# Attention with beacon keys and a quick-GELU MLP: order of the first loads, engine of the first masks, share of the copies

## The chip, the core and the metric

The kernel runs on one core of a Trainium2 chip. The core has a matmul engine (TensorE, PE in the profile), a vector engine (VectorE, DVE), a scalar engine for exp, GELU and copies (ScalarE, ACT), a general engine (GpSimd, POOL) and a queue engine that only issues transfers (SyncE, SP). Each runs its own list of instructions in order and waits for the others by semaphores. DMA transfers can be issued by SyncE, ScalarE and GpSimd; those of GpSimd may change the type on the way, from float32 in memory to float16 on the chip.

The metric is the time of one execution in microseconds. Before the change it is 367.99 us, the median of 5 runs (367.88 to 368.15).

## The reference

Eight batches, eight heads, 576 tokens of 64 features. Each head attends to 16 beacon keys, which every token sees, and causally to its own 576 keys. The result, all heads of a token side by side, goes through a two-layer MLP with x times sigmoid(1.702 x) between.

```python
B, H, S, Nb, D = (8, 8, 576, 16, 64)
k_all = concatenate([beacon_k, k], axis=2)
v_all = concatenate([beacon_v, v], axis=2)
scores = matmul(q, k_all.T) / sqrt(D)
scores = where(causal, -1e9, scores)        # beacon columns are never masked
a = exp(scores - scores.max(-1))
a /= a.sum(-1) + 1e-09
x = matmul(a, v_all)                        # to [B * S, H * D] = [4608, 512]
h = x @ w_in                                # 512 -> 2048
out = (h * sigmoid(1.702 * h)) @ w_out      # 2048 -> 512
```

## The kernel before, in words

**Pairs.** The unit of attention is a pair of heads: four pairs in each of eight batches, steps i = 0 to 31. For one pair, `qk_chunk` (L322) computes transposed scores (keys on partitions, queries along the row) in four chunks `CH` (L288), two heads each. `exp_chunk` (L340) turns a chunk into float16 weights E with ScalarE, and `mask_chunk` (L351) sets the weights above the diagonal to zero: one instruction for each of five diagonal blocks of a pair, on VectorE (a minimum with the tile `keep`) or on GpSimd (`affine_select`). Then TensorE multiplies E with V. A constant part of the V tile, set by `ones` (L100), makes row sums in the same way.

**Two ways to the normalized result.** The first four pairs (`NBOTH`) use `av_both` (L421), and VectorE reads the sums and products straight from PSUM (`z_turn_both`, `z_recip`, `z_back`, `norm_both`). Later pairs use `av_half` (L389); a copy `av_out` (L456) on VectorE or ScalarE takes the products out of PSUM, and VectorE does the rest (`z_turn`, `z_recip`, `z_back`, `norm`). The result is the MLP's input `xT`.

**q and k.** They are needed with features on partitions. For batches 0 and 1 they are loaded by `load_qk6` (L143), transposed by TensorE (`tr_pe`, L185) and copied out of PSUM (`tr_pe_out`, L196). In batch 0, heads 0 and 1 are an exception: `load_f32` (L151) loads them as float32 on the queues of SyncE (k) and ScalarE (q), and `cast_f32` (L162) makes float16 of them. Batches 2 to 7 are loaded by `load_qk` (L112), turned in 32 by 32 blocks on VectorE (`tr_squares`), put in order by VectorE or GpSimd (`tr_order`), written to memory and read back by SyncE (`tr_write`, `tr_place`).

**Beacons.** `load_bk6` (L170) and `cast_bk6` (L178) bring the beacon keys of batches 0 and 1; `load_bk` (L123, eight small transfers on SyncE) and `cast_bk` (L135) those of batches 2 to 7, at the kernel's start.

**MLP.** The 4608 tokens are nine groups of 512. `mlp1` (L511, matmuls at L516) makes 16 blocks of the hidden layer, each followed by a GELU on ScalarE; `mlp2` (matmuls at L538) makes four blocks of output, copied out by `mlp2_out` (L551 on VectorE, L549 on ScalarE) and stored by SyncE. Group g starts after the scores of pair `ends[g]` - 1, so the first group follows pair 4.

**What sets the order.** Every piece of work is a `Work` (L561) with the engines that may run it, a duration, a key (its due time in steps), the works it needs, and works that must start before it (`after`). `Buf` and `rings` (L573, L578) stand for the buffers in turn. `issue` (L964) is a planner that runs while the program is built: it takes again and again the work that could start first by its own clock, by key among equals, and for a work with several engines the one that would finish first, with a penalty `BIAS` (L765, L995) in microseconds: VectorE's is 0.5 up to its clock 45, ScalarE's 0.7 after. The order in which the works are taken is the program's order on each engine's list. So a changed duration or penalty can move any work. `first_loads` (L620) holds batches 0 and 1; the V loads are at L738, w_in and w_out at L744 and L745. Throw-away matmuls (`warm`, L1041) fill gaps of TensorE up to the planner's clock 60.

```python
c = (t, 0 if w.mode == mode == 1 else 1, w.key)
...
eng = min(w.opts, key=lambda e: max(t, free[e]) + w.opts[e] + BIAS[t > 45].get(e, 0))
```

Of the kernel before, what the change touches and what calls it, by code (L numbers as in the profile page):

```python
# [9 lines left out]
F16 = mybir.dt.float16  # L10
# [6 lines left out]
def kernel(  # L17
# [75 lines left out]

    w1t = cst.tile([P, NKP, DFF], F16, tag="w1", name="w1")
# [48 lines left out]
    def load_qk6(b, h0, h1, w):  # L143
        if b not in nat6:
            nat6[b] = gp.tile([TP, 2, H, TR * D], F16, tag="g", name="g")
        nc.gpsimd.dma_start(  # L146
            out=nat6[b][:, w, h0:h1, :],
            in_=(q, k)[w][b, h0:h1].rearrange("h (p t) d -> p h (t d)", t=TR),
        )

    def load_f32(w, eng):  # L151

        s = op_.tile([P, 2, S], F32, tag="O", name="O")
        stg[w] = s
        dict(SP=nc.sync, ACT=nc.scalar)[eng].dma_start(
            out=s.rearrange("p x s -> p (x s)")[0:TP, 0 : 2 * TR * D].rearrange(
                "p (h c) -> p h c", h=2
            ),
            in_=(q, k)[w][0, 0:2].rearrange("h (p t) d -> p h (t d)", t=TR),
        )  # L160

    def cast_f32(w, eng):  # L162
        if 0 not in nat6:
            nat6[0] = gp.tile([TP, 2, H, TR * D], F16, tag="g", name="g")
        copy[eng](
            out=nat6[0][:, w, 0:2, :].rearrange("p h c -> p (h c)"),
            in_=stg[w].rearrange("p x s -> p (x s)")[0:TP, 0 : 2 * TR * D],
        )
# [152 lines left out]

    def qk_chunk(i, ci):  # L322
        b, p = divmod(i, NPAIR)
        qT, kT = qTs[b % 2], kTs[b % 2]
        sc = pss.tile([P, 2, 512], F32, tag="s", name="s")
        scs[(i, ci)] = sc
        o = 0
        for (j, a, e) in CH[ci]:
            for x in range(2):
                r = 64 * x  # L330
                nc.tensor.matmul(  # L331
                    sc[:, x, o : o + e - a],
                    kT[r : r + 64, p, j * P : (j + 1) * P],
                    qT[r : r + 64, p, a:e],
                    start=True,
                    stop=True,
                )
            o += e - a
# [244 lines left out]
    SPL, CAP = 2.0, 2.0  # L583
    NBOTH = 4
# [9 lines left out]
    bkB = None  # L594
    pk = {}
    trp = {}
    mkeep = Work("POOL", 0.3, -4.95, make_keep)
    midn = Work("POOL", 0.6, -5.95, lambda: make_identity(nc, ident))

    bk6, stw, cst0 = {}, {}, {}  # L600
    stb = {w: Buf("O") for w in (1, 0, "bk")}
    stw[1] = Work("SP", 0.6, -9, lambda: load_f32(1, "SP"), alloc=stb[1], dma=0.7)
    stw[0] = Work("ACT", 0.6, -9, lambda: load_f32(0, "ACT"), alloc=stb[0], dma=0.7, after=[stw[1]])
    for b in range(NB2):
        ob = Buf("osb")
        x = Work("SP", 0.6, -8 + b, lambda b=b: load_bk6(b), alloc=ob, dma=0.1, after=[stw[1]])
        bk6[b] = Work(
            dict(ACT=0.6, DVE=0.6) if b else dict(ACT=0.6), 0, (-8, 1.5)[b],
            lambda eng, b=b: cast_bk6(b, eng), [x],
        )  # L610
        use(ob, bk6[b])
    g0 = Buf("g")
    for w in (1, 0):
        cst0[w] = Work(
            {("DVE", "ACT")[w]: 0.85}, 0, -8.5 - 0.1 * w, lambda eng, w=w: cast_f32(w, eng),
            [stw[w]],
        )
        use(stb[w], cst0[w])

    def first_loads(b):  # L620
        k0 = 4 * b
        kl = (-6, -4.4)[b]
        gb6 = g0 if b == 0 else Buf("g")
        lds = {(0, 1): cst0[1], (0, 0): cst0[0]} if b == 0 else {}
        got = []
        for (h0, h1) in ((2, 4), (4, H)) if b == 0 else ((0, 4), (4, H)):
            for w in (1, 0):
                x = Work(
                    "POOL", 0.7, kl + 0.1 * h0 + 0.02 * (1 - w) + (h0 == 4),
# [6 lines left out]
        if b == 0:  # L636
            for x in cst0.values():
                x.after.append(got[0])
# [31 lines left out]
        if b == 0:  # L670
            bk6[1].after.append(pk[(0, 0, 1)])

    for b in range(B):
# [5 lines left out]
        for g in range(2) if b >= NB2 else ():  # L679
            for w in (1, 0):  # L680
# [17 lines left out]
                for e in range(2):  # L698
                    cp.append(Work(
                        dict(DVE=0.8, POOL=1.3), 0, k0,  # L700
# [5 lines left out]
                if w == 1:  # L706
                    if bkB is None:
                        ld4 = [
                            Work(
                                "SP", 1.2, -6 + x, lambda x=x: load_bk(x),  # L710
                                alloc=stb["bk"] if x == 0 else None, dma=0.2,
# [3 lines left out]
                        for x, y in zip(ld4, ld4[1:]):  # L715
                            y.after.append(x)
                        bkB = [Work(dict(ACT=0.85, DVE=0.85, POOL=0.9), 0, 3, cast_bk, ld4)]
                        use(stb["bk"], *bkB)
# [46 lines left out]
    BIAS = dict(DVE=0.5), dict(ACT=0.7)  # L765
    avs = []
    evs = {}
    for i in range(NSTEP):
# [5 lines left out]
        for c in range(len(CH)):  # L774
            s_ = Buf("s")
            qk_ = Work(
                "PE", CHW[c] / 2400 + 0.05, i + (0, 0.01, 0.4, 0.41)[c],
                lambda i=i, c=c: qk_chunk(i, c),
                [pk[(b, p, 0)], pk[(b, p, 1)], pk[b]] if b < NB2
# [17 lines left out]
            mk = Work(  # L797
                dict(DVE=0.46 * nm, POOL=0.41 * nm), 0, i + 0.3,
                lambda eng, i=i, c=c: mask_chunk(i, c, eng), [ex, mkeep],
            )  # L800
            use(Eb, mk)
# [6 lines left out]
        if i < NBOTH:  # L808
            for z in (1, 0):
                for half in range(2):  # L810
# [4 lines left out]
                        "PE", sum(hi - lo for (j, lo, hi, col) in mm) / 2400 + 0.15,  # L815
                        i + 1.05 + 0.2 * (1 - z) + 0.1 * half,
                        lambda i=i, half=half, z=z: av_both(i, half, z),
                        [r for j in js for r in ready[j]] + vb_, alloc=ub[(half, z)],
# [71 lines left out]
    bkB[0].after.append(exps[0][3])  # L890
# [73 lines left out]
    def issue():  # L964
# [7 lines left out]
        while todo:  # L972
            best = None
            for w in todo:
# [20 lines left out]
                eng = min(w.opts, key=lambda e: max(t, free[e]) + w.opts[e] + BIAS[t > 45].get(e, 0))  # L995
# [15 lines left out]
            if w.key >= 1e6 and t < 7:  # L1011
                d = 0.43
# [65 lines left out]
```

The softmax here doesn't subtract the row's maximum and nothing guards it: scores larger than these inputs give would overflow.

## Time and profile before

| | |
|---|---|
| time, median of 5 runs | 367.99 us (367.88 to 368.15) |
| time of the profiled execution | 367.99 us |
| its span in the profile | 366.3 us |
| TensorE busy | 354.8 us, 97% |
| VectorE busy | 249.5 us, 68% |
| ScalarE busy | 228.4 us, 62% |
| GpSimd busy | 152.8 us, 42% |
| start of the first group's MLP (L516) | 35.02 us |
| start of its second layer (L538) | 58.90 us |
| copies out of PSUM after AV (L459) | 84 on VectorE, 440 ns each; 28 on ScalarE, 428 ns each |
| copies out of PSUM after the MLP | 30 on VectorE, 6 on ScalarE |
| masks | 12 on VectorE, 148 on GpSimd |

The page sums up one execution: busy time of each engine, forty equal slices of the span with a digit for tenths busy, and the chain of work that ended last, which goes back from the last instruction to what released it at each step. A line of a timeline is: start, duration, engine, line of the kernel, operation, output and input, number of instructions, and in brackets how long the engine had been idle before and what ended that. A matmul counts as busy from issue to its modelled end, so a busy TensorE isn't one at its peak. The span doesn't hold the launch: 1.7 us lie around it. "Landing" of a transfer is the time from its issue to its completion.

### The profile page before, as it was taken

What the parts mean: (1) busy time and instruction counts of PE and PEld (TensorE: products, weight loads), DVE (VectorE), ACT (ScalarE), POOL (GpSimd) and SP (SyncE); (2) the same over time, 40 slices, a digit from 0 to 9 for tenths busy, and PEclk for the clock granted to TensorE, in tenths of its full rate; (3) what the DMA queues carried; (4) which work ended last, traced back from release to release, by engine and by line L of the source; (5) the groups of instructions that cost most, each with busy time, mean ns of one, the idle gap of its engine ahead of it and who ended that gap; (6) DMA issues with size and microseconds to landing.
All of it is one profiled execution on the core that took longest, in us unless ns stands there. A gap on an engine that the chain in (4) does not pass through costs nothing.

```text
span 366.3 us, 6133 instructions
## 1 busy us (share of the span) xinstructions
PE 354.8 (97%) x2349; PEld 177.5 (48%) x2349; DVE 249.5 (68%) x421; ACT 228.4 (62%) x335; POOL 152.8 (42%) x264
## 2 busy tenths in 40 slices
PE   7889999999999999999999999999999999999995
PEld 3465444444444444544455864544444454444442
DVE  5556499999999986999699949972995183010021
ACT  4769787658765776776857675677658724616200
POOL 9668567593469245734375236611430010000000
PEclk9969999999999999999999999999999999999999
DMA  9999999995799545994479437921100011000012
GB/s 144 155 206 186 188 237 233 225 107 103 196 237 173 124 132 151 127 167 132 127 109 148 160 120 136 142 80 32 59 30 29 2 57 57 2 29 29 30 57 86
DMA packets 69788, 43.41 MB, mean 119 GB/s; under 512 B 42624, under 2 KB 62080, under 8 KB 69760
## 3 DMA queue, kind: packets, MB, share of 16 engines
q0 software_dynamic: 49152, 18.19, 49.0%
q1 hardware_dynamic: 20400, 24.55, 21.1%
q8 instruction: 18, 0.29, 0.3%
q10 hardware_dynamic: 208, 0.29, 0.3%
q14 instruction: 10, 0.08, 0.1%
HBM read 44.60 MB, written 16.61 MB: 167 GB/s over the span
## 4 chain that ended last, share of the span: by engine, by line
PE 86%; DVE 4%; ACT 3%; DMA 3%; POOL 2%; issue 1%; DVEq 0%; POOLq 0%
PE u L516 34%; PE u L538 34%; PE u L401 9%; PE s L331 7%; DMA g<-in_q_dram 3%; ACT E L344 2%; PE u L430 1%; POOL vb L221 1%; DVE xT L489 1%; PE u L190 1%; DVE rz L480 1%; DVE zt L470 1%; DVE osb L551 1%; DVE O L459 1%; POOL g L146 1%
## 5 line engine op out<-in xcount | busy, mean ns | idle before, releaser
L344 ACT ACTIVATE E<-s 128x1024 f16<-128x1024 f32 (+3 forms) x128 | 103.5, 865 | 48.9 <-PE s L331 47.0
L538 PE MATMUL u<-w,g 128*128 128x512 f16 x576 | 129.2, 379 | 0.5 <-DVE O L459 0.4
L516 PE MATMUL u<-xT,w 128*128 128x512 f16 (+1 forms) x640 | 126.0, 358 | 0.0
L528 ACT ACTIVATE g<-u 128x512 f16<-128x512 f32 x144 | 85.2, 597 | 42.8 <-PE u L516 42.5
L367 POOL TENSOR_SCALAR_AFFINE_SELECT E<-E 128x256 f16<-128x256 f16 (+2 forms) x148 | 63.6, 449 | 83.0 <-ACT E L344 82.7
L516 PEld LDWEIGHTS <-w 128*128 128x128 f16 x640 | 62.1, 98 | 61.3 <-issue 0.9
L538 PEld LDWEIGHTS <-g 128*128 128x128 f16 x576 | 54.5, 98 | 65.3 <-issue 3.6
L551 DVE COPY osb<-u 128x512 f32<-128x512 f32 x30 | 20.5, 683 | 65.3 <-PE u L538 65.0
L459 DVE COPY O<-u 128x240 f32<-128x240 f32 (+1 forms) x84 | 34.8, 440 | 24.4 <-PE u L401 22.1
L262 POOL COPY t<-sq 128x576 f16<-128x576 f16 x21 | 26.7, 1272 | 49.2 <-DVE sq L253 42.9
L401 PE MATMUL u<-E,vb 128*128 128x240 f16 x392 | 46.8, 266 | 0.2
L489 DVE TENSOR_TENSOR xT<-O,rz 64x576 f16<-64x576 f32 x56 | 44.2, 790 | 0.8
L470 DVE STREAM_TRANSPOSE zt<-O 64x576 f32<-64x576 f32 x56 | 43.1, 770 | 1.4
L401 PEld LDWEIGHTS <-vb 128*128 128x128 f16 x392 | 32.2, 97 | 17.4 <-issue 8.0
L331 PE MATMUL s<-qT,kT 64*128 64x80 f16 (+5 forms) x384 | 37.5, 288 | 2.3 <-ACT E L344 1.4
L253 DVE STREAM_TRANSPOSE sq<-n 128x576 f16<-128x576 f16 x48 | 34.8, 747 | 7.0 <-DMA n<-in_k_dram 6.7
L221 POOL DMA_DIRECT2D vb<-in_v_dram x40 | 34.4, 868 | 3.8 <-DMA w<-in_moe_w_in_dram 3.0
L262 DVE COPY t<-sq 128x576 f16<-128x576 f16 x27 | 27.5, 1019 | 0.3
L331 PEld LDWEIGHTS <-kT 64*128 64x128 f16 x384 | 13.1, 95 | 27.1 <-issue 19.0
L480 DVE STREAM_TRANSPOSE rz<-rt 128x576 f32<-128x576 f32 x32 | 24.4, 763 | 0.6
L459 ACT COPY O<-u 128x336 f32<-128x336 f32 (+1 forms) x28 | 10.7, 428 | 2.9 <-PE u L401 2.7
L1043 PE MATMUL u<-wu 128*128 128x512 f16 x29 | 10.8, 477 | 1.3 <-DVE wu L1036 1.3
(44 smaller groups left out, 126.9 us busy)
## 6 DMA issues: line engine op xcount, KB each, us to landing
out_dram<-osb SPq DMA_DIRECT2D x36, 256.0 KB, 2.1
d<-t SPq DMA_DIRECT2D x12, 296.0 KB, 3.2
kT<-d SPq DMA_DIRECT2D x12, 296.0 KB, 3.4
n<-in_k_dram POOLq DMA_DIRECT2D x12, 288.0 KB, 4.8
n<-in_q_dram POOLq DMA_DIRECT2D x12, 288.0 KB, 5.9
d<-t SPq DMA_DIRECT2D x12, 288.0 KB, 2.5
qT<-d SPq DMA_DIRECT2D x12, 288.0 KB, 3.2
vb<-in_v_dram POOLq DMA_DIRECT2D x24, 128.0 KB, 5.3
```

What stands on the lines that cost most here:

```text
L221: nc.gpsimd.dma_start(out=vb[r : r + hi - lo, j, :, 0:D], in_=v[b, :, lo:hi, :].rearrange("h n d -> n h d"),)
L262: copy[eng](out=tqk[(b, g, w)][:, e, o : o + S].rearrange("p (r t) -> p r t", t=TPP), in_=sqs[(b, g, w)][:, :, e, :].rearrange("p t r -> p ...
L331: nc.tensor.matmul(sc[:, x, o : o + e - a], kT[r : r + 64, p, j * P : (j + 1) * P], qT[r : r + 64, p, a:e], start=True, stop=True,)
L344: nc.scalar.activation(out=Es[i][:, :, choff[ci] : choff[ci] + w], in_=scs[(i, ci)][:, :, 0:w], func=AFT.Exp, scale=0.125,)
L367: nc.gpsimd.affine_select(out=blk, in_=blk, compare_op=ALU.is_ge, fill=0.0, base=mc, pattern=[[0, 2], [1, w]], channel_multiplier=-1,)
L401: nc.tensor.matmul(u[:, lo:hi], vb[0:kw, j, :, :].rearrange("r h c -> r (h c)")[:, o : o + 2 * D], E[0:kw, x, col : col + hi - lo], start= ...
L459: copy[eng](out=Os[i][:, x, AQ[half] : AQ[half + 1]], in_=avu[(i, x, half)][:, :])
L470: nc.vector.transpose(zst[i][0][64 * x : 64 * x + 64, :, :], Os[i][64 * (1 - x) : 64 * (1 - x) + 64, x, :])
L489: vec[eng].tensor_tensor(out=xT[r : r + 64, p, c : c + S], in0=Os[i][r : r + 64, x, :], in1=zst[i][2][r : r + 64, :], op=ALU.mult,)
L516: nc.tensor.matmul(u[:, o : o + w], w1t[:, kp, nt * P : (nt + 1) * P], xT[:, kp, m : m + w], start=(kp == 0), stop=(kp == NKP - 1),)
L528: nc.scalar.activation(out=gts[g][:, nt, :], in_=hu[(g, nt)][:, :], func=AFT.Gelu_apprx_sigmoid)
L538: nc.tensor.matmul(o[:, :], gts[g][:, nt, mt * P : (mt + 1) * P], w2t[:, nt, :], start=(nt == 0), stop=(nt == NNT - 1),)
```

## The change

- The float32 loads of heads 0 and 1 and their casts are taken out. Instead GpSimd's first two transfers load k and q of these heads as float16, ahead of the identity matrix (`midn`). The rest of batch 0 is loaded by two heads at a time, where it was two and then four.
- The beacon load of batch 1 comes after pair 0's third exp, and the eight loads of the later batches after the first exp of pair 2 (`BKE`). The cast of batch 1's beacons may be planned earlier, and the cast of batch 0's may also run on VectorE.
- The masks of the first five pairs (`NDM`) run on VectorE only.
- A tile `neg` is made on VectorE from `keep`, and `keep` is made earlier. It belongs to an optional way of masking by matmuls, which `NMASK = 0` leaves off for all pairs; the tile is made all the same, and the scores of batches 0 and 1 are planned behind it.
- The planner's penalty on ScalarE after its clock 45 (now called `TB`) goes from 0.7 to 0.3. Its estimate of `av_both` loses 0.09 us, and the sums of the first pairs need only the constant part of V in the plan. The throw-away matmuls count as slow up to its clock 5, where it was 7.

```diff
+    neg = cst.tile([P, P + Nb], F16, tag="neg", name="neg")
+    def make_neg():
+        nc.vector.tensor_scalar_add(neg, keep, -65504.0)
...
-    def load_f32(w, eng):
...
-    def cast_f32(w, eng):
...
+    def pe_mask(i, ci):
+        return i < NMASK and ci in CMASK
...
+    BKE = 2
+    NDM = 5
+    NTP = 9
+    NMASK = 0
+    CMASK = (0, 1, 2, 3)
+    TB = 45
...
-    mkeep = Work("POOL", 0.3, -4.95, make_keep)
-    midn = Work("POOL", 0.6, -5.95, lambda: make_identity(nc, ident))
-    stw[1] = Work("SP", 0.6, -9, lambda: load_f32(1, "SP"), alloc=stb[1], dma=0.7)
-    stw[0] = Work("ACT", 0.6, -9, lambda: load_f32(0, "ACT"), alloc=stb[0], dma=0.7, after=[stw[1]])
+    mkeep = Work("POOL", 0.3, -5.6, make_keep)
+    mneg = Work("DVE", 0.2, -5, make_neg, [mkeep])
+    midn = Work("POOL", 0.6, -5.97, lambda: make_identity(nc, ident))
...
-        x = Work("SP", 0.6, -8 + b, lambda b=b: load_bk6(b), alloc=ob, dma=0.1, after=[stw[1]])
+        x = Work("SP", 0.6, -8, lambda b=b: load_bk6(b), alloc=ob, dma=0.1)
+        bkl.append(x)
         bk6[b] = Work(
-            dict(ACT=0.6, DVE=0.6) if b else dict(ACT=0.6), 0, (-8, 1.5)[b],
-            lambda eng, b=b: cast_bk6(b, eng), [x],
+            dict(ACT=0.6, DVE=0.6), 0, -8, lambda eng, b=b: cast_bk6(b, eng), [x]
         )
...
-        for (h0, h1) in ((2, 4), (4, H)) if b == 0 else ((0, 4), (4, H)):
+        for (h0, h1) in ((0, 2), (2, 4), (4, 6), (6, H)) if b == 0 else ((0, 4), (4, H)):
             for w in (1, 0):
                 x = Work(
-                    "POOL", 0.7, kl + 0.1 * h0 + 0.02 * (1 - w) + (h0 == 4),
+                    "POOL", 0.7, kl + 0.1 * h0 + 0.02 * (1 - w) + (b == 0) * (h0 >= 4) + (b == 1) * (h0 == 4),
...
-        if b == 0:
-            bk6[1].after.append(pk[(0, 0, 1)])
...
-    BIAS = dict(DVE=0.5), dict(ACT=0.7)
+    BIAS = dict(DVE=0.5), dict(ACT=0.3)
...
-                [pk[(b, p, 0)], pk[(b, p, 1)], pk[b]] if b < NB2
+                [pk[(b, p, 0)], pk[(b, p, 1)], pk[b], mneg] if b < NB2
...
-            mk = Work(
-                dict(DVE=0.46 * nm, POOL=0.41 * nm), 0, i + 0.3,
+            mk = ex if pe_mask(i, c) else Work(
+                dict(DVE=0.46 * nm, **({} if i < NDM else dict(POOL=0.41 * nm))), 0, i + 0.3,
...
-                        "PE", sum(hi - lo for (j, lo, hi, col) in mm) / 2400 + 0.15,
+                        "PE", sum(hi - lo for (j, lo, hi, col) in mm) / 2400 + 0.06,
...
-                        [r for j in js for r in ready[j]] + vb_, alloc=ub[(half, z)],
+                        [r for j in js for r in ready[j]] + (vb_[-1:] if z else vb_), alloc=ub[(half, z)],
...
-    bkB[0].after.append(exps[0][3])
+    bkl[1].after.append(exps[0][2])
+    bkl4[0].after.append(exps[BKE][0])
...
-            if w.key >= 1e6 and t < 7:
+            if w.key >= 1e6 and t < 5:
```

## The prediction

> **What bounds the kernel now.** I read the page first: the busy shares, the forty slices, the chain of work that ended last.
>
> ```profile
> PE 354.8 (97%) x2349; PEld 177.5 (48%) x2349; DVE 249.5 (68%) x421; ACT 228.4 (62%) x335; POOL 152.8 (42%) x264
> PEclk9969999999999999999999999999999999999999
> DMA  9999999995799545994479437921100011000012
> PE 86%; DVE 4%; ACT 3%; DMA 3%; POOL 2%; issue 1%; DVEq 0%; POOLq 0%
> ```
>
> TensorE carries 86% of the chain, so the question is where the other 14% lies. The chain in order of time puts most of it ahead of 65 us:
>
> ```profile
> 8.60 10.59 DMA g<-in_q_dram
> ...
> 35.09 13.93 PE u L516 x64
> ...
> 65.39 3.61 PE u L538 x16
> ```
>
> From 65 us on the chain is matmul after matmul with a few tenths between. Ahead of the first MLP (35.09 us) TensorE has only the transposes and four pairs of heads to do, and the third slice shows its clock at six tenths. So the prize is the first 35 us and the 30 us behind them. The timeline of ScalarE from the start shows the hole:
>
> ```profile
> 5.09 0.83 ACT L165 CAST g<-O 96x768 f16<-96x768 f32 x1 [2.55 <-DMA O<-in_k_dram]
> ...
> 8.94 3.31 ACT L344 ACTIVATE E<-s 128x1024 f16<-128x1024 f32 x4 [1.30 <-PE s L331]
> 14.49 0.83 ACT L136 CAST bk<-O 128x768 f16<-128x768 f32 x1 [2.24 <-DMA O<-in_beacon_k_dram]
> 15.23 3.12 ACT L344 ACTIVATE E<-s 128x1024 f16<-128x1024 f32 x4
> ...
> 26.74 3.32 ACT L344 ACTIVATE E<-s 128x1024 f16<-128x1024 f32 x4
> ```
>
> The exps of pair 1 could follow those of pair 0 at 12.25 us; they stand behind a cast that waits for the late beacons. After them pair 2 waits for its q (issued 8.60, landed 19.2, the chain's DMA piece). Pair 3's exps start at 26.74, end at 30.06, and the MLP starts 5.0 us later.
>
> The second stretch is the first MLP's end (49.0) to the first second-layer block (58.90 to 62.5). The list of DMA issues there and VectorE's timeline say what else is near:
>
> ```profile
> w<-in_moe_w_out_dram POOLq DMA_DIRECT2D x1, 512.0 KB, 18.5
> ```
>
> That is the last quarter of w_out, issued at 41.7, landed at 60.2. The block reads it after three quarters of its 3.5 us, at 61.5: only 1.3 us of slack. VectorE idles 6.67 us until 41.38 (a k load of batch 2), then is busy 4.8 of every 5 us to 85.
>
> **What the skill says.** The Trainium skill, "DMA: Bandwidth & Descriptors", section "Issuing engines are not separate DMA queues": loads from SyncE, ScalarE and GpSimd share the same 16 engines and interleave. The trace agrees: batch 0's four last V chunks, with beacons beside them, land over 5.5 us (10.2 to 15.7), batch 1's last four in about 3.6 (at the 0.9 to 1.2 us between their landings at 37.8, 39.0, 40.0, 40.4). So the beacons cost 1.9 us of transfer, wherever they stand. The same page, "Anatomy of one DMA — SWDGE (gpsimd) path", gives some 2.0 us fixed per transfer plus bytes; here, in quiet, 16 KB took 2.8 and 288 KB 4.5 us from issue, so it is a little dearer. "TensorE: Matmul & The Clock Gate", "What's actually happening": an idle window halves the clock. The trace shows 0.57 at 20 to 25 us, and 32 matmuls of L430 in 2.89 us there, 1.67 later.
>
> **The change, part by part.**
>
> *First loads (faster).* Before, k of heads 0 and 1 lands at 0.81 + 4.3 = 5.1 and passes a cast of 0.83; transposes start at 5.97, and q's cast ends at 6.45. After, GpSimd issues both first, at 0.81 and 1.5, already as f16. For 144 KB between the quiet 16 KB (2.8) and 288 KB (4.5) I take 3.6: landed at 4.4 and 5.1. Upper bound: the 5.3 and 5.8 of the present second pair, landing 6.1 and 7.3, which loses up to 0.9. I take the quiet value, since the load is first. Both casts go (0.83 and 0.84). Exps of pair 0 start about 1.2 earlier, at 7.7. The identity moves behind two issues of 0.7: ready at 2.8, still before 4.4. The first beacon load is now first on SyncE: between 2.8 and 4.7 us, plus cast 0.62, transpose 0.27 and copy 0.21, it is ready by 4.7 to 6.6, under q's copy.
>
> *neg.* One VectorE instruction of 128x144; nearest rows 0.18 (memset of keep) and 0.27 (mask). 0.1 to 0.3, hidden in VectorE's 1.35 us wait before 5.61; without that cover 0.2. The mask matmuls aren't issued, since NMASK is 0. keep moves ahead of V: 0.33 later for V.
>
> *Beacons behind.* The 2.24 wait and the 0.83 cast leave ScalarE between pairs 0 and 1. Exps of pair 1 start at 11.1, not 15.23. The eight later beacon issues (SyncE, 4.7 us together) now follow pair 2's first exp, when SyncE's queue is empty; the transfer (1.9) and the cast (0.83) fall on another engine's order near 25 us, and could stall one there by 1 to 2 us.
>
> *Loads by two heads.* GpSimd's order becomes k, q, identity, k, q, keep, V, then heads 4 and 5, 6 and 7, batch 1. V's first chunk lands near 8.8 (issue 5.2 plus the quiet 3.6), the last at 12.4, against 15.7. At 1.4 us per 288 KB (the 20.6 and 22.0 landings of batch 1), k and q of heads 4 and 5 land at 13.2 and 13.9; the later q of heads 6 and 7, behind one k load of batch 1 by its key, at 16.8, against 19.2 for all. Two more issues of 0.7 on GpSimd are hidden: it waits for landings there anyway (the 0.5 to 1.4 waits in its timeline). Pair 2: 13.9, transposes 0.45, copy 0.75, score and wait as for pair 0 (0.94): exps at 16.1.
>
> *Masks on VectorE.* Some 20 masks at 0.27 move: 5.4 us, against 8.6 at 0.41 to 0.43 on GpSimd. A pair on VectorE is then 1.0 + 0.27 + 0.78 + 0.82 (sums and norm) + 1.25 (five masks) + 0.75 (one copy) = 4.9 us; on ScalarE 3.32 + 0.65 + a wait of 0.37 = 4.34, the spacing now between pairs 3 and 4. So VectorE becomes the pace: pair 3's exps at 16.1 + 4.9 = 21.0, end 24.3, MLP at 24.3 + 5.0 = 29.3. I say 29.5, that is 5.5 us earlier. Behind a mask on VectorE stand the norms, and the AV matmuls wait for it; this is in the 4.9.
>
> *What is late next.* All DMA from 19 to 60 us is one backlog, so w_out moves only with the sum of its queue: V's lead of 3.3, less the 1.9 of beacons that come back, is 1.4; counting the loads behind V at 1.4 per 288 KB throughout gives 2.7. I take 2.0: last quarter at 58.2. The second-layer block could start at 58.9 - 5.5 = 53.4, would read that quarter at 56.0, and waits 2.2 there: it ends at 58.2 + 0.9 = 59.1, against 62.5. **Gain 3.4.** VectorE's batch 2 work starts 2 us earlier too.
>
> *Copies shared evenly (penalty of ScalarE 0.7 to 0.3).* The 84 + 30 copies on VectorE (0.41, 0.69) partly move to ScalarE (0.44, 0.59), which has 48.9 us of idle time before exps. No table load falls due: a copy at 57.76 stands between exps without one. TensorE has about 6 us of waits after 65 us (301 us, less 8 MLP first layers of 13.82, 35 blocks of 3.46 and some 25.5 pairs of 2.45); VectorE ends few. I take 0.2 gain, bounds -1 and +4. The planner's shorter AV estimate and the sums that no longer wait for V in its plan: 0 to 0.5, taken as nothing, being hidden under V's earlier landing.
>
> **Sum:** 3.4 + 0.2 = 3.6. Profiled: span 366.3 - 3.6 = 362.7, and 1.7 lies around it (367.99 against 366.3), so **364.4**; the profiled run's 367.99 is also the median.
>
> **Rivals.** *The transfers take it back:* if w_out's last quarter stays at 60.2, only its slack of 1.4 is won: 366.6. For it: the DMA row of nines through 82 us; against: two f32 loads halve their written bytes. *All is kept:* if w_out lands by 56, the 5.5 stay: 362.5. For it: the write-outs that compete at 45 to 60 us may start behind the AV work; against: the 18.5 us landing. *Slower:* copies on ScalarE stand ahead of an exp for which TensorE waits. At five places (101.94, 140.91, 179.35, 217.97, 256.42) an exp is on the chain; a copy there costs 0.44 to 0.59. From 3.6 / 0.44, eight such over 28 pairs use up the gain; twelve give 3.6 - 5.3, so 369.7. Against it: the other exps find ScalarE waiting 2.1 to 2.6 us for TensorE. *No change:* masks on VectorE and a stalled cast eat the start: 368.0.
>
> **How the numbers follow.** Forecast 0.45 (363.2 to 365.6), transfers 0.16 (365.6 to 367.2), all kept 0.18 (361 to 363.2), no change 0.07, slower 0.14. Range 361.4 to 367.4, which leaves out the slower case, most of no change and the tip of "all kept". Within 0.2% (0.74 us) a measurement can't tell it from no change: faster 0.79, same 0.07, slower 0.14.
>
> **What would show it.** Right: pair 0's exps near 7.7, pair 1's directly behind at 11, no cast of bk between; the last V of batch 0 near 12.4; clock full at 20 us; L516 from 28 to 31; the first L538 longer than 3.5 us with a DMA wait on w_out. Wrong: L516 later than 33; a wait of VectorE or ScalarE on the beacons before 30; transposes waiting past 6 us on the first k; more ScalarE pieces on the chain after 65 us.

## The result and the profile after

The changed kernel takes 369.36 us (median of 21 runs, 367.93 to 370.62), against 368.11 us (41 runs, 367.49 to 368.88) for the kernel before on the same chips. The ratio is 1.0035, 95% interval 1.0026 to 1.0043: **slower by a third of a per cent**. The forecast was 364.4 us, and the range (361.4 to 367.4) doesn't hold the result. The profiled execution took 370.05 us, its span is 368.3 us, 2.0 more than before; it lies 0.7 us above the median, so its trace stands for the slower half of the runs.

The page of the changed kernel, its busy shares, the clock and DMA rows of its forty slices, and the shares of the chain:

```profile
PE 352.3 (96%) x2348; PEld 175.4 (48%) x2348; DVE 242.3 (66%) x428; ACT 232.7 (63%) x349; POOL 148.7 (40%) x246
...
PEclk9999999989999999999999999999999999999999
DMA  9999999999389944894479447921100011000012
...
PE 78%; DMA 3%; POOL 2%; ACT 1%; DVE 1%; issue 1%; DVEq 0%; POOLq 0%
```

The third slice is now at full clock, as forecast. TensorE and VectorE are busy for less time than before (354.8 and 249.5), and the kernel is longer all the same: TensorE's time without work went from 11.5 to 16.0 us. The eighth and ninth slices (64 to 83 us) lie beyond the stretch in which I had looked for the gain, and the ninth has a dent in the clock that the kernel before hasn't.

**The first 35 us went as meant, up to the last step.** ScalarE's timeline of the changed kernel:

```profile
8.51 3.50 ACT L348 ACTIVATE E<-s 128x1024 f16<-128x1024 f32 x4 [1.06 <-PE s L322]
...
13.02 2.85 ACT L348 ACTIVATE E<-s 128x1024 f16<-128x1024 f32 x3
...
26.89 1.02 ACT L348 ACTIVATE E<-s 128x1024 f16<-128x1024 f32 x1
27.81 0.82 ACT L142 CAST bk<-O 128x768 f16<-128x768 f32 x1
```

The hole before pair 1 is gone: its exps start at 13.02 (before 15.23), those of pairs 2, 3 and 4 at 18.38, 23.11 and 26.89 (before 21.52, 26.74 and 31.08). The last norm that the first MLP needs ends at 31.70, 3.0 us earlier than before (34.71). The cast of the later beacons found them landed and waited for nothing.

This execution was a quick one up to here. In three of the experiments below, the engines' lists up to this point are those of the changed kernel, and pair 2's exps began at 20.80, 21.16 and 21.13 in place of 18.38. Their first MLP started at 34.37, 34.42 and 34.46 all the same. The first of the three:

```profile
20.80 3.26 ACT L348 ACTIVATE E<-s 128x1024 f16<-128x1024 f32 x4
```

So the gain of the pairs isn't steady, and what came of it at the MLP didn't depend on it. Why the pairs were later in these executions isn't known.

But TensorE's timeline of the changed kernel shows that only a part arrives at the MLP, and what becomes of that part:

```profile
33.16 0.45 PE L177 MATMUL u<-ident,g 96*64 96x96 f16 x12 [2.89 <-DMA g<-in_k_dram]
34.29 13.98 PE L520 MATMUL u<-xT,w 128*128 128x512 f16 x64
...
58.00 3.63 PE L542 MATMUL u<-w,g 128*128 128x512 f16 x16
64.11 3.61 PE L542 MATMUL u<-w,g 128*128 128x512 f16 x16
72.29 5.30 PE L542 MATMUL u<-w,g 128*128 128x512 f16 x16 [1.90 <-DVE O L463]
80.10 3.63 PE L542 MATMUL u<-w,g 128*128 128x512 f16 x16
85.49 13.98 PE L520 MATMUL u<-xT,w 128*128 128x512 f16 x64
```

The reader is to see three things. TensorE stands in its list at the transposes of pair 6's k (batch 1, heads 4 and 5), whose load landed at 33.1, and so the MLP starts at 34.29 instead of 35.02. The first two second-layer blocks start 0.90 and 1.28 us earlier than before (58.90, 65.39). The third starts 0.87 later (before 71.42), the fourth 2.68 later (77.42), and the second MLP 2.05 later (83.44). The lines of the kernel before for the third block and the second MLP:

```profile
71.42 3.61 PE L538 MATMUL u<-w,g 128*128 128x512 f16 x16
...
82.91 0.60 PE L331 MATMUL s<-qT,kT 64*128 64x512 f16 x8
83.44 13.99 PE L516 MATMUL u<-xT,w 128*128 128x512 f16 x64
```

The sum by steps against before: -1.28 at the second block; +2.15 from there to the third (8.18 against 6.03); +1.81 from the third to the fourth (7.81 against 6.00); -0.63 to the second MLP (5.39 against 6.02); together +2.05. The last step is no gain of speed: the eight score matmuls that stand ahead of the second MLP before (0.60 us) stand behind it in the changed kernel, at 99.40. After that the lag falls to 1.28 at the sixth MLP and is 1.90 from the seventh on; the span is 2.0 longer.

VectorE's timeline shows what the third block waited for:

```profile
40.70 2.16 DVE L240 STREAM_TRANSPOSE sq<-n 128x576 f16<-128x576 f16 x3 [8.80 <-DMA n<-in_k_dram]
...
49.67 0.78 DVE L463 COPY O<-u 128x240 f32<-128x240 f32 x2
...
66.71 0.78 DVE L484 STREAM_TRANSPOSE rz<-rt 128x576 f32<-128x576 f32 x1
69.61 0.78 DVE L240 STREAM_TRANSPOSE sq<-n 128x576 f16<-128x576 f16 x1 [2.12 <-DMA n<-in_k_dram]
70.31 1.49 DVE L493 TENSOR_TENSOR xT<-O,rz 64x576 f16<-64x576 f32 x2
71.83 0.72 DVE L463 COPY O<-u 128x240 f32<-128x240 f32 x2
```

At 67.5 VectorE reaches the first turn of batch 3's k (its transposing in 32 by 32 blocks), which has not landed, and stands for 2.12 us. Behind it in the list are pair 6's norm and pair 7's first two copies; the third block can't start before the first copy frees a PSUM buffer. In the kernel before, the planner had put this turn behind pair 7's copies:

```profile
70.96 1.24 DVE L459 COPY O<-u 128x240 f32<-128x240 f32 x3
...
74.25 0.72 DVE L253 STREAM_TRANSPOSE sq<-n 128x576 f16<-128x576 f16 x1
```

There it came 5.5 us after its k had landed (68.78), and could hold up nothing. The changed plan has it ahead of the norm and the copies. The chain in order of time says the same from the other side:

```profile
57.11 12.40 DMA n<-in_k_dram
...
69.61 0.78 DVE sq L240
...
71.83 0.42 DVE O L463
...
72.29 5.30 PE u L542 x16
```

That load is issued at 57.11 (0.6 earlier than before, 57.74), takes 12.4 us (before 11.0) and lands 0.7 later than before. And the wait costs more than its length: the block after it takes 5.30 us instead of 3.6. The table by stretches (bounds, length, busy time and instructions of the five engines, TensorE's clock, DMA share, GB/s) for that block and for the next:

```profile
72.30:76.00 3.70, 3.70 (x10) 1.38 (x10) 3.64 (x7) 0.00 (x0) 3.69 (x6) 0.54 0.97 128
80.10:83.73 3.63, 3.63 (x22) 1.56 (x20) 3.21 (x7) 1.72 (x2) 3.19 (x8) 1.00 1.07 130
```

After 1.90 us without work TensorE ran 3.6 us at half clock. The price of the wait is 1.9 plus 1.7.

### The profile page after: what moved, and what is told of

Same layout as the page of the kernel before. It is cut to its first block, busy times and chain, and to the rows that moved or that the text cites. A ratio compares the mean times of both kernels' runs of the same rounds, so it can differ in the third digit from the quotient of the medians.

```text
span 368.3 us, 6138 instructions
## 1 busy us (share of the span) xinstructions
PE 352.3 (96%) x2348; PEld 175.4 (48%) x2348; DVE 242.3 (66%) x428; ACT 232.7 (63%) x349; POOL 148.7 (40%) x246
## 4 chain that ended last, share of the span: by engine, by line
PE 78%; DMA 3%; POOL 2%; ACT 1%; DVE 1%; issue 1%; DVEq 0%; POOLq 0%
PE u L542 33%; PE u L520 30%; PE u L405 9%; PE s L322 6%; DMA n<-in_k_dram 3%; ACT E L348 1%; POOL vb L208 1%; POOL t L249 1%; DVE sq L240 0%; DVE xT L493 0%; DVE osb L555 0%; POOL vb L205 0%; POOL E L371 0%; DVE O L463 0%; DVEq L240 0%
## 5 line engine op out<-in xcount | busy, mean ns | idle before, releaser
L542 PE MATMUL u<-w,g 128*128 128x512 f16 x576 | 130.9, 383 | 1.9 <-DVE O L463 1.9
L348 ACT ACTIVATE E<-s 128x1024 f16<-128x1024 f32 (+3 forms) x128 | 105.5, 870 | 32.6 <-PE s L322 30.7
L532 ACT ACTIVATE g<-u 128x512 f16<-128x512 f32 x144 | 84.1, 598 | 40.0 <-PE u L520 39.3
L371 POOL TENSOR_SCALAR_AFFINE_SELECT E<-E 128x256 f16<-128x256 f16 (+2 forms) x126 | 57.4, 468 | 92.4 <-ACT E L348 92.3
L555 DVE COPY osb<-u 128x512 f32<-128x512 f32 x24 | 16.6, 691 | 66.3 <-PE u L542 66.2
L463 DVE COPY O<-u 128x240 f32<-128x240 f32 (+1 forms) x79 | 33.7, 449 | 30.8 <-PE u L405 28.1
L553 ACT COPY osb<-u 128x512 f32<-128x512 f32 x12 | 7.0, 586 | 29.1 <-PE u L542 29.1
L249 DVE COPY t<-sq 128x576 f16<-128x576 f16 x27 | 24.7, 913 | 0.3
L463 ACT COPY O<-u 128x336 f32<-128x336 f32 (+1 forms) x33 | 13.2, 421 | 2.4 <-PE u L405 2.4
```

The source lines that it names most:

```text
L249: copy[eng](out=tqk[(b, g, w)][:, e, o : o + S].rearrange("p (r t) -> p r t", t=TPP), in_=sqs[(b, g, w)][:, :, e, :].rearrange("p t r -> p ...
L348: nc.scalar.activation(out=Es[i][:, :, choff[ci] : choff[ci] + w], in_=scs[(i, ci)][:, :, 0:w], func=AFT.Exp, scale=0.125,)
L371: nc.gpsimd.affine_select(out=blk, in_=blk, compare_op=ALU.is_ge, fill=0.0, base=mc, pattern=[[0, 2], [1, w]], channel_multiplier=-1,)
L463: copy[eng](out=Os[i][:, x, AQ[half] : AQ[half + 1]], in_=avu[(i, x, half)][:, :])
L532: nc.scalar.activation(out=gts[g][:, nt, :], in_=hu[(g, nt)][:, :], func=AFT.Gelu_apprx_sigmoid)
L542: nc.tensor.matmul(o[:, :], gts[g][:, nt, mt * P : (mt + 1) * P], w2t[:, nt, :], start=(nt == 0), stop=(nt == NNT - 1),)
```

## The experiments

Theory A, formed from the two traces: the sign comes from one place, VectorE's turn of batch 3's k ahead of pair 7's copies, for which TensorE has now come too early. Theory B: the copies on ScalarE delay exps and cost a little everywhere. Beside them stand the questions why the start gave so little, and whether the beacons were held back at all.

**One turn moved behind the copies.** After the planning, the first turn of batch 3's k is moved behind pair 7's copies; nothing else. (The lists `trw` and `outs` only remember these works; later diffs leave them and `move` out.)

```diff
...
     order = issue()
+
+    def move(ws, behind):
+        for w in ws:
+            order.remove(w)
+        at = max(order.index(w) for w in behind) + 1
+        order[at:at] = ws
+
+    move(trw[(3, 0, 1)][:1], outs[7])
```

> The changed kernel with one VectorE instruction moved: the first block transpose of batch 3's k is put behind the four PSUM copies of pair 7, all other lists as they are. Theory A (the loss is made where VectorE waits in order for that k, 2.1 us, with the norm and the copies behind it, so that TensorE's third second-layer block waits 1.9 us for PSUM and then runs at half clock): the wait of TensorE on a VectorE copy near 70 us is gone, that block takes 3.6 us instead of 5.3, and the kernel takes 2.5 to 3.6 us less than the changed one, 366 to 367, a little below the kernel before. Theory B (copies on ScalarE slow the exps all along): nothing of that spacing changes, within 0.7 us of 369.4.

Measured: 367.27 us (14 runs, 366.16 to 369.6), ratio to before 0.9989 (0.9974 to 1.0004). VectorE's timeline of this kernel:

```profile
67.36 1.52 DVE L493 TENSOR_TENSOR xT<-O,rz 64x576 f16<-64x576 f32 x2
68.91 0.72 DVE L463 COPY O<-u 128x240 f32<-128x240 f32 x2
69.55 0.77 DVE L474 STREAM_TRANSPOSE zt<-O 64x576 f32<-64x576 f32 x1
70.35 0.78 DVE L240 STREAM_TRANSPOSE sq<-n 128x576 f16<-128x576 f16 x1
```

and TensorE's:

```profile
70.31 3.63 PE L542 MATMUL u<-w,g 128*128 128x512 f16 x16
76.44 3.63 PE L542 MATMUL u<-w,g 128*128 128x512 f16 x16
81.89 8.37 PE L520 MATMUL u<-xT,w 128*128 128x512 f16 x38
```

The copies come 2.9 us earlier, the turn finds its data, and the third block runs at full clock. The second MLP starts at 81.89, 3.6 before the changed kernel's and 1.55 before the kernel before's (0.6 of the 1.55 are the score matmuls that now stand behind it). By the ratios, 1.0035 less 0.9989, this one place is worth 0.46%, 1.7 us. Theory A holds for the sign; the 2.5 to 3.6 us that I expected were too much, since I took them from the changed kernel's slow profiled run. This one's profiled run (366.44) is the second fastest of the 14, and two of the 14 took 369.6, as long as the changed kernel. No trace says why.

**Pair 6's transposes behind the first MLP layer.** The transposes of its k and their copy are moved behind the MLP's 16 blocks.

```diff
...
+    move([trp[(1, 2, 1)], pk[(1, 2, 1)]], gl0)
```

> The changed kernel with TensorE's 12 transposes of k for pair 6 (and their copy on ScalarE) put behind the first MLP layer of group 0. Theory: at the start the gain is lost because TensorE stands in order at these transposes until the k of batch 1, heads 4 to 7, lands at 33.1 us, while the last norm the MLP needs is done at 31.7. Then the first MLP layer starts at about 32, 2.3 us earlier. If the loss from 66 to 76 us is a separate one, or w_out's landing near 60 us is the next bound, at most 1 us of that reaches the end: 368 to 369.4. If the start sets the end, 367.

Measured: 368.52 us (21 runs), ratio 1.0023 (1.0015 to 1.0031). TensorE's timeline:

```profile
32.49 13.98 PE L520 MATMUL u<-xT,w 128*128 128x512 f16 x64
...
50.16 1.17 PE L177 MATMUL u<-ident,g 96*64 96x96 f16 x24 [2.13 <-DVE O L463]
60.20 3.63 PE L542 MATMUL u<-w,g 128*128 128x512 f16 x16
```

The MLP starts 1.8 us earlier and the first block 2.2 later. VectorE's first copy of pair 4 is at 49.74, where it was at 49.67: it stands behind the turning of batch 2, which begins when its k lands. So TensorE came earlier only to wait 2.13 for that copy, and its clock was at half after it until about 56.5; it was busy all that time, so this held the first block back too. The start of the MLP isn't what the copies ahead of the first block hang on; the landing of batch 2's k is (its turning begins at 40.81, in the changed kernel at 40.70).

**The beacons really held.** In the changed kernel SyncE's timeline reads:

```profile
1.73 3.79 SPq L134 DMA_DIRECT2D O<-in_beacon_k_dram x8
```

(before: from 2.21). The eight loads go out earlier, not later. `bkl4[0].after.append(exps[BKE][0])` moves the work in the planner's clock; SyncE's own list has nothing with a wait ahead of it, so the chip issues at once. Here a small write into the staging tile, from pair 2's weights, makes SyncE wait in fact.

```diff
         if x == 0:
             stg["bk"] = op_.tile([P, 2, S], F32, tag="O", name="O")
+            nc.scalar.copy(out=stg["bk"][0:SQ, 0, 0:8], in_=Es[BKE][0:SQ, 0, 0:8])
```

> The changed kernel with a small ScalarE copy out of pair 2's weights into the beacon buffer, so that SyncE really waits for pair 2's first exp before the eight later beacon loads; it adds nothing else, and what it writes is overwritten by the loads. Theory: in the changed kernel these loads still go out at 1.7 to 5.5 us, because the planner's order leaves nothing with a wait ahead of them on SyncE's list. Held, the last V of batch 0 lands near 13.5 instead of 15.5 and pair 2's exps start 1 to 1.5 us before 18.4; the transposes of pair 6 still wait for their k (33.1, within 0.5, since the same transfers come before it), so the first MLP layer starts within 0.7 us of 34.3 and the end moves by less than 1 us: 368.4 to 370.4. If the early beacons were what took the forecast gain, the MLP would start 2 us earlier and the end would follow to about 367.5.

Measured: 372.12 us (5 runs), ratio 1.0105 (1.0089 to 1.0121): outside what I expected. The first loads do gain: k and q of heads 0 and 1 take 3.3 us each (3.9 and 4.4 in the changed kernel), pair 0's exps start at 7.20 (8.51), pair 1's at 11.35 (13.02), and V's last chunk lands at 14.41 (15.42). But the loads, issued from 19.6 on, meet w_in and batch 1, land at 34.7, and ScalarE waits with pair 4's last three exps behind the cast:

```profile
34.72 0.83 ACT L143 CAST bk<-O 128x768 f16<-128x768 f32 x1 [5.69 <-DMA O<-in_beacon_k_dram]
```

Pair 6's k lands at 34.90 (33.11), and the MLP starts at 38.72. What the change says of the beacons costs 0.7% more than what it does.

**Held, but with the cast moved to VectorE behind pair 3's norm** (with the turn moved as in the first experiment), to part the waiting cast from the transfer.

```diff
...
+    bkB[0].eng = "DVE"
+    move(bkB, norms[3])
```

> The changed kernel with the first block transpose of batch 3 behind pair 7's copies, with the eight later beacon loads really held until pair 2's first exp, and their cast moved from ScalarE to VectorE behind pair 3's norm, where VectorE is idle. Against the run that held the beacons alone (372.1) it tells what the 4.4 us there are: if it is ScalarE's 5.7 us wait in front of the cast, the MLP starts again near 35 (k of batch 1 lands at 35.1 instead of 33.1, since the beacons now compete with w_in) and the time is 367 to 369. If held beacons cost by their transfer alone, it stays above 370.5. A forecast gain of 3 us from holding them (364.4) is not expected.

Measured: 370.80 us (6 runs), ratio 1.0072 (1.0058 to 1.0086). The cast blocks no exp now, and the MLP still starts at 37.41. TensorE's timeline:

```profile
35.44 0.69 PE L178 MATMUL u<-ident,g 96*64 96x96 f16 x12 [6.20 <-DMA g<-in_k_dram]
```

It stays above 370.5, where I had put the case that the transfer alone costs: pair 6's k lands 2.3 us later than in the changed kernel, batch 2's k at 42.6 instead of 40.7.

**The penalty back to 0.7**, in the changed kernel.

```diff
-    BIAS = dict(DVE=0.5), dict(ACT=0.3)
+    BIAS = dict(DVE=0.5), dict(ACT=0.7)
```

> The changed kernel with the planner's penalty on ScalarE back at 0.7, so that the even sharing of copies is undone and the rest stays. Theory A: the sharing isn't dear in itself; what matters is where the order puts VectorE's first transpose of batch 3 against the copies. In this plan it still stands ahead of a norm and copies, so most of the wait stays and the time is 368 to 370. Theory B (copies on ScalarE slow the exps): the time falls to 366.5 or below, and the start's 0.7 us show.

Measured: 370.51 us (5 runs), ratio 1.0069 (1.0056 to 1.0082), so about 1.2 us slower than the changed kernel, and 0.5 us above theory A's range. The turn of batch 3's k still stands ahead of the copies and waits 2.26 us, so it isn't the penalty that put it there. With more copies on VectorE (87 after AV, for 79) the third block is later still:

```profile
71.50 0.71 PE L405 MATMUL u<-E,vb 128*128 128x336 f16 x5 [1.90 <-DVE osb L555]
73.36 4.94 PE L542 MATMUL u<-w,g 128*128 128x512 f16 x16 [0.61 <-DVE O L463]
```

Theory B, a fall to 366.5 or below, is refuted here: the sharing helps where VectorE is late.

**The sharing alone**, in the kernel before.

```diff
-    BIAS = dict(DVE=0.5), dict(ACT=0.7)
+    BIAS = dict(DVE=0.5), dict(ACT=0.3)
```

> The kernel before with the planner's penalty on ScalarE after its clock 45 at 0.3 instead of 0.7: the even sharing alone. Theory A (sharing itself is about free, the order decides): within 1 us of the kernel before, and any loss sits at one place near 60 to 85 us. Theory B (copies on ScalarE slow the exps all along): 1 us or more slower, with the spacing of the later MLP layers (38.5 us) longer by 0.2 or more.

Measured: 368.50 us (13 runs), ratio 1.0011 (1.0003 to 1.0019), as theory A has it: 0.4 us slower. Its cost is again one place, the fourth block; after it the groups are as long as before or a little shorter (38.3 us on the mean from the second MLP to the seventh, against 38.4).

```profile
78.19 3.61 PE L538 MATMUL u<-w,g 128*128 128x512 f16 x16 [1.08 <-DVE O L459]
```

**No penalty at all** (0 in place of 0.3), with the turn moved as in the first experiment.

> The changed kernel with batch 3's first turn behind pair 7's copies and the penalty on ScalarE 0 in place of 0.3, so that more copies run on ScalarE. Theory A (VectorE is the tight one from 41 to 85 us and copies on ScalarE delay no exp): second MLP at 81.0 to 81.8 (81.89 in e1_turn_later), time 366.0 to 367.3. Theory B (a copy on ScalarE stands ahead of an exp that TensorE waits for): spacing of the later MLPs over 38.6, 367.6 to 369.5.

Measured: 376.74 us (6 runs), ratio 1.0254 (1.0226 to 1.0282). The page counts 47 copies after AV and 36 after the MLP on ScalarE (33 and 12 in the changed kernel). The time is far outside both ranges. The second MLP starts at 87.68, 5.8 later than with the turn moved alone, and TensorE's waits name a part of the price:

```profile
PE s L322 <- ACT E L348: 6.1, 12, 1.2
PE u L520 <- DVE O L463: 2.6, 1, 2.6
```

From MLP to MLP it is now 39.2 us (38.4 with the turn moved alone). The rival "copies on ScalarE stand ahead of an exp" is real; it counts between 0.3 and 0, and was not seen between 0.7 and 0.3.

**The masks back** (`NDM = 0` in the changed kernel), and **the masks alone** in the kernel before.

```diff
-    NDM = 5
+    NDM = 0
```

> The changed kernel with the masks of the first five pairs on either engine again (NDM = 0); all else as changed, though the planner's later order moves with it. Theory A (the masks on VectorE shorten the pairs, but the start of the first MLP is set by the transposes of pair 6's k, landing at 33.1): exps of pairs 2 to 4 are 0.5 to 1.5 us later than 18.38, 23.11, 26.89, the first MLP starts within 0.6 of 34.29, and batch 3's k is still waited for ahead of pair 7's copies: 368.6 to 370.2 us. Theory B (the masks are what brought the pairs forward): pair 4's exps at 29 or later, first MLP at 35.5 or later, little or no wait at 70 us.

```diff
-                dict(DVE=0.46 * nm, POOL=0.41 * nm), 0, i + 0.3,
+                dict(DVE=0.46 * nm, **({} if i < 5 else dict(POOL=0.41 * nm))), 0, i + 0.3,
```

> The kernel before with the masks of the first five pairs on VectorE alone. Theory A (before, the pairs wait for beacons and for pair 2's q, not for masks): exps of pair 3 no more than 0.7 earlier than 26.74, first MLP 34.4 to 35.4, time within 0.6 us of the kernel before. Theory B (masks are worth something by themselves): first MLP at 34.0 or earlier, and the time 0.8 or more lower, or higher where the new order puts a wait ahead of a copy.

Measured: 369.62 us (6 runs), ratio 1.0047 (1.0032 to 1.0062), and 370.74 us (6 runs), ratio 1.0078 (1.0063 to 1.0094). With the masks back, pair 4's exps start at 27.86 (26.89) and the time is the same within the intervals. In both the planner's order did more than the masks. With them back it puts pair 6's transposes behind the MLP by itself, which then starts at 33.11, and it loses the lead elsewhere, with a 1.7 us wait for a copy at 85.57. Alone in the kernel before it puts the transposes of pair 6's q and of pair 7's k ahead of the MLP:

```profile
35.95 0.69 PE L190 MATMUL u<-ident,g 96*64 96x96 f16 x12 [1.88 <-DMA g<-in_q_dram]
...
38.14 16.06 PE L516 MATMUL u<-xT,w 128*128 128x512 f16 x64
```

Pair 3's exps came 1.2 us earlier (25.51), and the MLP 3.1 later. The 1.2 are not the masks' for sure: with nothing changed at the start, they came at 25.98 in the run of the sharing alone and at 25.61 in that of the next experiment. Neither expectation had a wait in these places; with the masks back the time is in theory A's range, but the wait for batch 3's k, which it also foresaw, isn't there. So I can't give the masks a price of their own: it is under what the order around them decides.

**Before, with batch 3's turn moved early**, ahead of pair 6's norm, as the changed kernel has it:

```diff
...
     order = issue()
+    first = trw[(3, 0, 1)][0]
+    order.remove(first)
+    at = order.index(norms[6][0])
+    order[at:at] = [first]
```

> The kernel before with one VectorE instruction moved: the first block transpose of batch 3's k ahead of pair 6's norm and pair 7's copies, the place that it has in the changed kernel. There VectorE comes to it near 68.8 us, when that k has just landed (68.7), so it hardly waits. Theory A (what costs is the wait in order, and half clock after it, not the place or the 0.75 us itself): the third second-layer block starts at most 0.8 us later and the time is within 0.9 us of the kernel before. If the place alone makes the loss, 370 or more.

Measured: 369.54 us (5 runs), ratio 1.0033 (1.0021 to 1.0045). That is over theory A's 0.9 us and under the 370 of its rival, and it is as much as the whole change loses. In its profiled run (368.38 us) the turn, at 68.44, finds its data by a tenth of a microsecond (landed 68.34), the second MLP is 0.3 late and nothing else shows. The other four runs (369.50 to 369.68) are 1.1 us longer, and no trace says where. That the k landed after VectorE reached the turn in them is likely with so small a margin; it isn't shown. So the place of the turn makes a loss of this size in the kernel before too, where TensorE has no lead; the first experiment takes it away, this one puts it in.

**Both moves together**, and pair 4's first two copies on ScalarE.

```diff
...
+    move(trw[(3, 0, 1)][:1], outs[7])
+    move([trp[(1, 2, 1)], pk[(1, 2, 1)]], gl0)
+    for w in outs[4][:2]:
+        w.eng = "ACT"
```

> The changed kernel with three edits: the first block transpose of batch 3 behind pair 7's copies, the transposes of pair 6's k behind the first MLP layer of group 0, and pair 4's first two PSUM copies on ScalarE. Theory (VectorE's turning of batch 2, which can't start before that k lands at 40.7 us, holds pair 4's copies until 49.7 and so took back what the MLP gained): the MLP's first layer starts at 32.5, TensorE no longer waits 2.1 us for a VectorE copy behind it, and the first second-layer block ends near w_out's landing of 59.7 plus 0.9, some 60.6, which is 1 us ahead of the changed kernel; time 365.8 to 366.8. If the copies aren't what holds it, the block starts at 60 as with the transposes moved alone, and the time is about 368.5.

Measured: 368.17 us (14 runs, 366.43 to 369.06), ratio 0.9998 (0.9987 to 1.0010). The profiled run is the shortest of them: MLP at 31.48, first block at 57.47, second MLP at 81.87, no earlier than with the turn alone. It lies in the range that I expected; the median doesn't: all but one of the others are 1 to 2.6 us longer. Its trace has a TensorE wait of 2.64 us at 49.92 that did not halve the clock; that it does so in other runs would explain them, but no run was profiled in which it did.

**w_in's last half behind batch 1's second half**, so that pair 6's k lands before it is asked for, with the turn moved as in the first experiment.

```diff
...
+    lds1 = [w for w in order if w.eng == "POOL" and w.fn.__name__ == "<lambda>" and w.fn.__defaults__ and w.fn.__defaults__[:3] == (1, 4, 8)]
+    move(W1[2:], lds1)
```

> The changed kernel with batch 3's first turn behind pair 7's copies (as in e1_turn_later) and the last two quarters of w_in loaded behind k and q of batch 1's heads 4 to 7. Theory A (VectorE's turn of batch 2's k, landing at 40.7 with the whole of the queue, caps what an earlier MLP can win): the k lands near 28, the first MLP starts at 32.0 to 33.0, the turn stays at 40.5 to 41.0, first second-layer block 57.3 to 58.3, time 366.2 to 367.4, that is as e1_turn_later within 0.6. Theory B (the start of the MLP carries through): block at 56.5 or earlier, 365.0 to 366.0.

Measured: 367.23 us (19 runs, 366.58 to 367.89), ratio 0.9981 (0.9974 to 0.9987). This is the one version whose interval is wholly below the kernel before, by 0.7 us, and it is 0.5% below the changed kernel by the ratios. Pair 6's k lands at 29.09 and its transposes no longer wait for it (32.72), yet the MLP of the profiled run starts at 33.94, later than I expected, since its pairs ran later too (pair 2's exps at 20.89); batch 2's turn came at 41.31 and the first block at 58.67, both later than expected. That run is the longest of the 19, and with an MLP hardly earlier it is no test of what an earlier one is worth. The median is that of the first experiment; its spread is 1.3 us against 3.4.

## Why the prediction was wrong

**Pairs and clock: the pace was right.** The hole left ScalarE, pairs 1 to 4 followed each other at 5.4, 4.7 and 3.8 us (4.9 was my figure), the clock was full at 20 us, and `neg` showed nowhere. But pairs 1 to 3 began 1.9 to 2.3 us later than in the sum (13.02, 18.38 and 23.11 for 11.1, 16.1 and 21.0), and this was a quick execution. **First loads: half right.** GpSimd issued k and q at 1.36 and 2.11, not 0.81 and 1.5, and they took 3.9 and 4.4 us, not 3.6. Pair 0's exps came 0.4 us earlier, not 1.2. With the beacons really held both loads took 3.3 us and the exps began at 7.20 (7.7 was my figure), so this miss comes from the next step. (The 2.8 us for 16 KB in my reading was the longest of five such loads after 70 us; the others took 2.0 to 2.3.)

**"Beacons behind": the first step that failed.** I wrote that the eight issues "now follow pair 2's first exp". They went out from 1.73 on. I had read the order of the planner as a wait of the chip. V's last chunk landed at 15.42, not 12.4, and the lead that I gave to all later loads, 2.0 us, was 0.7: batch 2's turn began at 40.70 instead of 41.38. The beacons explain only a part of V's 3.0 us: with them held it landed at 14.41 and 14.64 in the two runs. The rest is my sum for V, whose first chunk took 5.8 us from its issue, and 4.9 with the beacons held, where I took the quiet 3.6. Nor do they cost 1.9 us "wherever they stand": early they cost V 0.8 to 1.0, late they cost pair 6's k 1.8 and 2.3. Holding them in fact costs 0.7% more, some 2.6 us.

**"MLP at 29.5": the second.** Of the 4.8 us by which it was late, 2.2 had gone when pair 3's norm ended (31.70). For the rest, the sum ended at pair 3's norm and left out what stands in TensorE's list between it and the MLP. That list asks for pair 6's k, which landed at 33.1. Before, with the norm at 34.71 and the k landed at 33.74, this load was covered; with the cover gone it set 34.29, whatever the pairs did (34.37 to 34.46 where pair 2 was 2.4 to 2.8 us later).

**"What is late next": wrong transfer.** It wasn't w_out's last quarter (landed at 59.6, in time for a block that began at 58.00), but batch 2's k at 40.7, through VectorE's turning and pair 4's copies at 49.7. The second experiment shows it: an MLP 1.8 us earlier moved those copies by 0.1. That is why the first block gained 0.9 and not 3.4.

**After 65 us: the sign.** I took 0.2 for the shared copies and nothing else. (The 6 us of waits that I put there were 5.0 in the trace of before.) The sharing moved only 11 copies, and its worth depends on the plan around it: taking it back costs the changed kernel about 1.2 us, and alone it costs the kernel before 0.4. The term that I put at nothing is the new order itself: it set the turn of batch 3's k ahead of a norm and pair 7's copies, where it stood behind them. There VectorE comes to it before the k is there. 2.1 us of wait, and a clock at half for 3.6 us, turned -1.28 at the second block into +2.68 at the fourth and +2.04 at the end. The lead brings VectorE there earlier (67.5 for 68.4 in the kernel before with the early turn), but the place costs as much there, without the lead (1.0033). None of the rivals had this mechanism; the "slower" one put it on ScalarE, where it was seen only at a penalty of 0. With the turn moved back the change is worth 0.9989 (0.9974 to 1.0004): a gain that can hardly be told from none, where 3.4 us were expected.

**What stays open:** which part of the change made the planner move the turn (not the penalty: with 0.7 back it stands there still); what the lead adds to the place; the price of the masks alone; why two runs of the kernel with the turn moved took 369.6 us; and why the timed runs of two of the experiments (the early turn before, both moves together) are for the most part 0.3 to 0.7% longer than their profiled run.

## What to carry to other kernels

A transfer planned "after" a work is held only if its engine's list has a wait ahead of it: look in the trace for where it was issued, not in the planner. When an early stage gets faster, go down each engine's list behind it, and for each instruction that needs a load compare the landing with the new time; what was covered by a microsecond or less is the next bound, and what stands behind it in the list pays as well. Compare the lists too: a work that was moved ahead of others can make them wait for its load. And a change of one cost in a planner that orders everything is two changes: test the part with the order held (move one work by hand) before giving it a price.

## What the runs showed of the hardware

A wait of TensorE of 1.9 to 2.9 us sometimes halves its clock and sometimes doesn't. After 1.90 us in the changed kernel the clock was 0.53 for 3.6 us, after 2.13 us in the second experiment 0.50 for some 6.3 us; after 2.89 us in the changed kernel (at 33.16), 2.64 us (both moves) and 2.61 us (no penalty) it was 1.00. The Trainium skill, "TensorE: Matmul & The Clock Gate", "What's actually happening", says that activity is watched in windows of some 3.4 us that run freely, so that the point of change varies between runs. Windows that run freely would let one wait be caught and a longer one not; that they do so here is argued, not shown. It gives "≥1 idle window" for the slow clock; here waits of well under 3.4 us were enough, and the measurement decides. So in these traces a wait of this length cost its own time, or nearly twice that (1.90 and then 1.7 us in the changed kernel). It could also make the spread of the runs, 2.7 us for the changed kernel against 1.4 for the kernel before, which has no wait over 0.5 us after 20 us. That isn't shown: the trace of the first experiment has no wait over 0.8 us after 5 us, and its runs spread over 3.4 us; whether its slow runs had such a wait isn't known.

GpSimd's float32 to float16 loads of 144 KB took 3.9 and 4.4 us from issue as the first of the queue, and 3.3 and 3.3 with the eight beacon loads held back: with the beacons beside them they took 0.6 and 1.1 us longer. The k loads of 288 KB in the kernel before took 4.5 us on the median after 85 us (3.9 to 5.7). Half the bytes took about three quarters of the time at best.
